# Keys turned by VectorE in 32x32 blocks, scores added from four shares, in a decode attention kernel

## The chip, the cores and the metric

The kernel runs on one core of one Trainium2 chip. The metric is the device time of one execution in microseconds (us), as the median of several runs. A profiled execution has a time of its own and a span, which goes from its first to its last instruction. The engines are TensorE (PE in the profile, its weight loads PEld), VectorE (DVE), ScalarE (ACT), GpSimd (POOL) and SyncE (SP), which here issues the large loads.

## What is computed

One decode step for two sequences: attention over a window of 4096 cached positions, with 32 query heads on 8 key/value heads of 128 elements, and a gate from a small gated MLP. All numbers are float32.

```python
W = min(4096, max(256, Sk // 4))                      # 4096
q = (x @ wq).reshape(B, Sq, Hq, Dh)                   # B = 2, Sq = 1, Hq = 32, Dh = 128
k = repeat(k_cache[:, :, Sk - W:, :], 4 heads each)
v = repeat(v_cache[:, :, Sk - W:, :], 4 heads each)
p = softmax((q . k) * Dh ** -0.5)
s = (p . v) @ wo
g = silu(gated_mlp(xn))
return x + s * g                                      # xn = layernorm(x) feeds both branches
```

## The kernel before

The loads are 89 MB: `w_in`, `w_out`, `wq`, sixteen key/value windows of 2 + 2 MB, and `wo`. They go through a ring of four slots (`slot`), all issued by SyncE in program order. A slot takes a new load when the work that read its old contents is done. The sixteen combinations of sequence and key/value head are called pairs, numbered n = 0 to 15; `load_kv(n)` puts a pair's keys and values into one slot, with position 32p + j in partition p, row j, so that each partition reads one contiguous piece. After the last pair, the ring takes `wo` in six loads.

Every engine runs its instructions in the order in which the program issues them (the class `InOrder` keeps it), so the order of the calls in the loop over `pairs` is the order on each engine. In the iteration of pair `cur`, with `prev` the pair before it and `old` the one before that, the kernel does this:

- `bias(prev)` (VectorE) and `probs(prev)` (ScalarE): the row maximum becomes the bias of the exponential, which also adds up its row (`l`).
- `transposes(cur, c)`, c = 0 to 7: TensorE transposes four 128x128 blocks of keys into a PSUM bank, and VectorE or ScalarE (`ON_ACT`) copies the bank to `kts`, one tile for each half r of the pair.
- `probs_t(prev, r)`: VectorE turns the probabilities in 32x32 blocks. `share_sum` and `weights` make the factors 1/sum.
- `scores(cur, r)`: four products, one for each quarter of the positions, each with a 32-column block of the queries `qT` as weights. The four write different quarters of the partitions of `s`, and run beside each other in the array.
- `collect(old)`: the outputs of `old` are added into `col`. When a set of heads is complete (SETS: heads 0 to 3, 4 and 5, 6 and 7 of each sequence) VectorE reduces `col` into `o1`.
- `pv(prev, r)`: probabilities times values, into `acc`; `row_max(cur)` (VectorE) and `share_max(cur)` (TensorE, into `mo`) stand around it, and `evacuate(prev)` (ScalarE) scales `acc` into `o`.

So row maximum and its shares come at the end of a pair's own iteration, and the exponential at the start of the next one. The tiles `s`, `mo` and `acc` exist once, `kts`, `o`, `p` and `pT` twice, the PSUM banks of `bank` three times.

After the loop come the bias, exponential and values of the last pair, `spread(i)`, which brings the outputs of a set into the layout for `wo`, and the product with `wo`: the first 24 rows by `wo_early` in 512-wide products into `part`, then `parts`, its copy in SBUF, is added up by products with `rowm` into `so`, where the last eight rows of `wo` go directly. `res` multiplies by the gate and adds x.

Ahead of the loop, the queries are projected (`queries(k)`, k = 0 to 3, into `pq`), copied by VectorE into `qs`, transposed by TensorE and copied into `qT`.

Of the kernel before, what the change touches and what calls it, by code (L numbers as in the profile page):

```python
# [9 lines left out]
F32 = mybir.dt.float32  # L10
# [6 lines left out]
G = 4  # L17
# [24 lines left out]
def kernel(  # L42
# [82 lines left out]
    qT = cst.tile([P, B * HKV, 32], F32, tag="qT", name="qT")  # L125
    nc.gpsimd.memset(qT, 0.0)
# [32 lines left out]
    dve.tensor_copy(same, free_ap(rowm, 0, [[0, G], [1, 32]]))  # L159
    heads = cst.tile([P, 32, REP], F32, tag="heads", name="heads")  # L160
# [101 lines left out]
    qs = sb.tile([P, NR, REP, DH], F32, tag="kts", name="qs")  # L262
    for r in range(NR):
        dve.tensor_copy(qs[:, r], pq[:, r, :].rearrange("p (i d) -> p i d", i=REP))
    for r in range(NR):
        pt = bank(f"qT_ps{r}", REP, G, 32)
        for i in range(REP):
            pe.transpose(pt[:, i].rearrange("p g c -> p (g c)"), qs[:, r, i, :], ident)
        for b in range(B):
            dve.tensor_copy(  # L270
                qT[:, b * HKV + r * G : b * HKV + r * G + G, ::8], pt[:, :, :, b].rearrange("p i g -> p g i")
            )
# [5 lines left out]
    NP = B * HKV  # L278
# [14 lines left out]
    ON_ACT = {2, 4, 5, 7}  # L293

# [3 lines left out]
    def transposes(p, c):  # L298
        r, q = divmod(c, 4)
        if q == 0:  # L300
            p.kt[r] = sb.tile([P, JH, P], F32, tag="kts", name=f"kts{p.n}_{r}")
        pk = bank(f"kt{p.n}_{c}", 4, P)
        for jj in range(4):
            pe.transpose(pk[:, jj, :], p.k[:, 4 * c + jj, :], ident)
        dst = p.kt[r][:, 4 * q : 4 * q + 4, :]
        if c in ON_ACT:
            act.activation(dst, pk, AF.Copy)
        else:
            dve.tensor_copy(dst, pk)

    def scores(p, r):
        if r == 0:
            p.s = ps.tile([P, NR, 512], F32, tag="s", name=f"s{p.n}")
        for g in range(G):
            pe.matmul(
                p.s[32 * g : 32 * g + 32, r, :], qT[:, p.n, :], p.kt[r][:, :, 32 * g : 32 * g + 32],
                start=True, stop=True,
            )
# [84 lines left out]
    for n in range(NP):  # L403
        p = Pair()
        p.n, p.kt = n, {}
        pairs.append(p)
    old = prev = None
    for cur in pairs:
        cur.k, cur.v = load_kv(cur.n)
        do(bias, prev)  # L410
        do(probs, prev)
        for c in range(4):
            do(transposes, cur, c)
        do(probs_t, prev, 0)
        do(transposes, cur, 4)
        do(transposes, cur, 5)
        do(probs_t, prev, 1)
        do(transposes, cur, 6)
# [104 lines left out]
```

## Time and profile before

| | |
|---|---|
| median of 3 runs (lowest, highest) | 219.39 us (219.15, 219.85) |
| the profiled execution: its time, its span | 219.26 us, 217.4 us |
| mean granted TensorE clock | 0.953 |
| busy: TensorE, its weight loads | 174.4 us, 105.9 us |
| busy: VectorE, ScalarE | 109.4 us, 80.5 us |
| share of the 16 DMA engines taken by SyncE's loads | 96.5% |
| read from HBM | 89.40 MB, 411 GB/s over the span |
| VectorE copies of keys out of PSUM | 64 of 680 ns, 42.2 us |
| ScalarE copies of keys out of PSUM | 64 of 597 ns, 36.8 us |
| score products | 256 records of 598 ns, 30.8 us |

The profile of one execution gives for each engine its busy time, the groups of instructions that cost most, with the mean duration of one, and what ended the idle time before them. All engine work is issued through one helper, so every group has the same line, L36, and is told apart by the tiles that it writes and reads (`kt<-ident,kv` writes `kt` and reads `ident` and `kv`). A float32 product makes two matmul records in the trace, a transpose one. Records of products that use different quarters of the array overlap, so their busy time is less than their number times their duration. In a table by windows, each row gives the start and end of a stretch, its length, busy time and instructions of the engines (PE, PEld, DVE, ACT, POOL), then the granted TensorE clock, the busy share of the DMA engines and GB/s. The chain of waits follows the execution back from its last instruction, at each step to what released it; its rows give start, length and what.

### The profile page before, as it was taken

What the parts mean: (1) busy time and instruction counts of PE and PEld (TensorE: products, weight loads), DVE (VectorE), ACT (ScalarE), POOL (GpSimd) and SP (SyncE); (2) the same over time, 40 slices, a digit from 0 to 9 for tenths busy, and PEclk for the clock granted to TensorE, in tenths of its full rate; (3) what the DMA queues carried; (4) which work ended last, traced back from release to release, by engine and by line L of the source; (5) the groups of instructions that cost most, each with busy time, mean ns of one, the idle gap of its engine ahead of it and who ended that gap; (6) DMA issues with size and microseconds to landing.
All of it is one profiled execution on the core that took longest, in us unless ns stands there. A gap on an engine that the chain in (4) does not pass through costs nothing.

```text
span 217.4 us, 3786 instructions
## 1 busy us (share of the span) xinstructions
PE 174.4 (80%) x1554; PEld 105.9 (49%) x1554; DVE 109.4 (50%) x259; ACT 80.5 (37%) x173; POOL 3.6 (2%) x17
## 2 busy tenths in 40 slices
PE   0179793977998979797977979797987899599973
PEld 0128520563663736455462736455472846384333
DVE  2411212284785737575665737575664557374201
ACT  5011203012563644435363544536363336444210
POOL 6000000000000000000000000000000000000000
PEclk9998579799999999999999999999999699969999
DMA  7999999999999999999999999999999999999980
GB/s 254 428 435 470 398 467 389 428 428 427 434 434 425 434 427 425 431 428 431 425 431 428 434 434 428 431 427 431 428 431 428 431 430 428 440 467 395 410 329 13
DMA packets 6096, 89.64 MB, mean 412 GB/s; under 512 B 686, under 2 KB 702, under 8 KB 1088
## 3 DMA queue, kind: packets, MB, share of 16 engines
q1 hardware_dynamic: 6060, 89.40, 96.5%
q8 instruction: 12, 0.20, 0.3%
q14 instruction: 4, 0.03, 0.0%
q10 hardware_dynamic: 20, 0.01, 0.0%
HBM read 89.40 MB, written 0.00 MB: 411 GB/s over the span
## 4 chain that ended last, share of the span: by engine, by line
DMA 68%; PE 27%; DVE 2%; ACT 1%; issue 1%; SPq 1%; ACTq 0%
DMA kv<-in_A_k_cache_dram 52%; DMA wq<-in_A_wq_dram 16%; PE kt L36 10%; PE s L36 4%; PE acc L36 4%; PE part L36 3%; PE q_ps L36 2%; PE y L36 1%; PE so L36 1%; PE col L36 1%; SPq L36 1%; ACT o L36 1%; DVE m L36 1%; ACT p L36 1%; PE oT_ps L36 0%
## 5 line engine op out<-in xcount | busy, mean ns | idle before, releaser
L36 PE MATMUL kt<-ident,kv 128*128 128x128 f32 x512 | 68.7, 287 | 17.5 <-DMA kv<-in_A_k_cache_dram 17.3
L36 PEld LDWEIGHTS kt<-ident,kv 128*128 128x128 f32 x512 | 58.2, 146 | 25.7 <-issue 18.0
L36 DVE COPY kts<-kt 128x512 f32<-128x512 f32 x64 | 42.2, 680 | 27.2 <-PE kt L36 18.1
L36 ACT ACTIVATE kts<-kt 128x512 f32<-128x512 f32 x64 | 36.8, 597 | 34.1 <-PE kt L36 34.1
L36 ACT ACTIVATE o<-acc,wd 128x128 f32<-128x128 f32 x64 | 18.3, 368 | 52.7 <-PE acc L36 36.0
L36 PE MATMUL s<-kts,qT 128*32 128x512 f32 x256 | 30.8, 598 | 0.0
L36 PE MATMUL acc<-kv,pT 128*16 128x512 f32 x256 | 30.4, 592 | 0.4 <-DVE pT L36 0.4
L36 DVE TENSOR_REDUCE m<-s 128x1 f32<-128x1024 f32 x16 | 19.5, 1221 | 13.5 <-PE s L36 13.5
L36 DVE STREAM_TRANSPOSE pT<-p 128x512 f32<-128x512 f32 x32 | 20.7, 685 | 0.2 <-ACT p L36 0.2
L36 ACT ACTIVATE p<-s,nb 128x1024 f32<-128x1024 f32 x16 | 18.1, 1132 | 3.7 <-DVE nb L36 3.7
L36 PE MATMUL q_ps<-wq,xnT 128*32 128x512 f32 x64 | 10.5, 789 | 5.5 <-DMA wq<-in_A_wq_dram 5.5
L36 PEld LDWEIGHTS acc<-kv,pT 128*16 128x16 f32 x256 | 7.8, 108 | 10.7 <-issue 9.8
L36 PEld LDWEIGHTS mo<-mg,same 128*128 128x128 f32 x32 | 4.8, 188 | 15.9 <-DVE mg L36 15.9
L36 PEld LDWEIGHTS s<-kts,qT 128*32 128x32 f32 x256 | 6.6, 108 | 10.0 <-ACT kts L36 7.8
L36 PE MATMUL z<-win,xnT 128*32 128x448 f32 x32 | 5.5, 862 | 4.4 <-DMA win<-in_B_w_in_dram 4.4
L36 PEld LDWEIGHTS col<-o,selw 128*32 128x32 f32 x128 | 4.1, 110 | 8.9 <-issue 8.9
L36 DVE TENSOR_REDUCE o<-col 128x32 f32<-128x128 f32 x6 | 1.7, 291 | 12.5 <-PE col L36 12.5
L36 PE MATMUL mo<-mg,same 128*128 128x4 f32 x32 | 6.2, 263 | 2.1 <-DVE mg L36 1.6
L36 DVE TENSOR_REDUCE nb<-mo 128x1 f32<-128x4 f32 x16 | 2.6, 162 | 9.9 <-PE mo L36 9.9
L36 PE MATMUL zT_ps<-rowm,z 128*128 128x2 f32 x28 | 6.6, 370 | 0.0
L36 PEld LDWEIGHTS zT_ps<-rowm,z 128*128 128x128 f32 x28 | 6.5, 325 | 0.0
L36 PE MATMUL col<-o,selw 128*32 128x128 f32 x128 | 6.5, 273 | 0.0
(98 smaller groups left out, 83.3 us busy)
## 6 DMA issues: line engine op xcount, KB each, us to landing
kv<-in_A_k_cache_dram SPq DMA_DIRECT2D x16, 2048.0 KB
kv<-in_A_v_cache_dram SPq DMA_DIRECT2D x16, 2048.0 KB, 25.4
wq<-in_A_wq_dram SPq DMA_DIRECT2D x2, 4096.0 KB, 34.1
wo<-in_A_wo_dram SPq DMA_DIRECT2D x1, 4096.0 KB
win<-in_B_w_in_dram SPq DMA_DIRECT2D x1, 3584.0 KB, 11.1
wo<-in_A_wo_dram SPq DMA_DIRECT2D x1, 2048.0 KB, 21.7
wout<-in_B_w_out_dram SPq DMA_DIRECT2D x1, 1792.0 KB, 15.0
wo<-in_A_wo_dram SPq DMA_DIRECT2D x1, 1024.0 KB
```

The costliest lines, as they stand in the source:

```text
L36: return self.tc.keep_in_program_order(call(*args, **kwargs))
```

## The change

Keys are no longer transposed by TensorE. `turn(p, q)` lets VectorE transpose the 32x32 blocks of eight rows of keys (128x1024) at once, from SBUF to SBUF, into the same `kts` tiles. What stands in partition 32g + d of a turned block is then element d of a quarter c of the head, for the positions of partition group g, so a product over all 128 partitions with the right weights mixes nothing only if the weights are zero outside one group: `qb` holds the queries spread in this way, with one 32-column block for each quarter c. `shares(p, r)` makes four products, one for each quarter of the head, into four quarters of the partitions of one bank `sh`; `keep` copies it to `ss` in SBUF (ScalarE); `scores(p, r)` is now a single product of `ss` with the 0/1 matrix `sums`, which adds the four quarters and puts the result where it was before. The queries go through ScalarE copies, VectorE transposes, a masked product (`qa`) and masked copies into `qb`, in place of TensorE transposes.

The order in the loop is new: `row_max` and `share_max` of `prev` and `collect(old)` come after the first turn of `cur`, and `bias` and `probs` of `prev` after the second. After the loop, `collect(old)` comes before the two `spread`s, `wo_early` takes a range of rows, so that four rows come ahead of the last `collect`, eight ahead of `spread(2)` and the others behind it, and the products with `parts` come after the first of the direct blocks.

```diff
--- before.py
+++ after.py
@@ -122,8 +122,10 @@
     nc.gpsimd.memset(ones, 1.0)
     hT = cst.tile([P, FT, 32], F32, tag="hT", name="hT")
     nc.gpsimd.memset(hT, 0.0)
-    qT = cst.tile([P, B * HKV, 32], F32, tag="qT", name="qT")
-    nc.gpsimd.memset(qT, 0.0)
+    qb = cst.tile([P, B * HKV, G, 32], F32, tag="qb", name="qb")
+    nc.gpsimd.memset(qb, 0.0)
+    sums = cst.tile([P, G, 4, 8], F32, tag="sums", name="sums")
+    nc.gpsimd.memset(sums, 0.0)
 
     rowm = cst.tile([P, 32], F32, tag="rowm", name="rowm")
     dve.tensor_reduce(rowm, ident.rearrange("p (g c) -> p c g", g=G), axis=AX.X, op=ALU.add)
@@ -157,6 +159,7 @@
 
     same = cst.tile([P, G, 32], F32, tag="same", name="same")
     dve.tensor_copy(same, free_ap(rowm, 0, [[0, G], [1, 32]]))
+    dve.tensor_copy(sums[:, :, :, 0], rowm[:, : G * REP].rearrange("p (g i) -> p g i", g=G))
     heads = cst.tile([P, 32, REP], F32, tag="heads", name="heads")
     dve.tensor_copy(heads, free_ap(rowm, 0, [[0, 32], [8, REP]]))
     diag = cst.tile([P, 4], F32, tag="diag", name="diag")
@@ -259,23 +262,38 @@
     dve.tensor_mul(gate, gate, y)
 
     queries(3)
-    qs = sb.tile([P, NR, REP, DH], F32, tag="kts", name="qs")
+
+
+    NP = B * HKV
+    HC = REP * G
+    qs = sb.tile([P, NR, 512], F32, tag="kts", name="qs")
+    qx = sb.tile([P, NR, HC, 32], F32, tag="kts", name="qx")
     for r in range(NR):
-        dve.tensor_copy(qs[:, r], pq[:, r, :].rearrange("p (i d) -> p i d", i=REP))
-    for r in range(NR):
-        pt = bank(f"qT_ps{r}", REP, G, 32)
-        for i in range(REP):
-            pe.transpose(pt[:, i].rearrange("p g c -> p (g c)"), qs[:, r, i, :], ident)
-        for b in range(B):
-            dve.tensor_copy(
-                qT[:, b * HKV + r * G : b * HKV + r * G + G, ::8], pt[:, :, :, b].rearrange("p i g -> p g i")
-            )
-
-
-
-
-
-    NP = B * HKV
+        act.activation(qs[:, r], pq[:, r], AF.Copy)
+        dve.transpose(qx[:, r].rearrange("p a b -> p (a b)"), qs[:, r])
+    xm = cst.tile([P, B, NR, G, HC], F32, tag="xm", name="xm")
+    for b in range(B):
+        dve.tensor_tensor(
+            xm[:, b], free_ap(qx, b, [[32 * HC, NR], [0, G], [32, HC]]), free_ap(grpm, 0, [[0, NR], [1, G], [0, HC]]),
+            op=ALU.mult,
+        )
+    qa = bank("qa", NP, REP, G)
+    pe.matmul(
+        qa.rearrange("p n i c -> p (n i c)"), same.rearrange("p g c -> p (g c)"), xm.rearrange("p b r g a -> p (b r g a)"),
+        start=True, stop=True,
+    )
+    for g in range(G):
+        dst = free_ap(qb, REP * g, [[G * 32, NP], [1, REP], [32, G]])
+        if g % 2:
+            act.activation(dst, qa, AF.Copy, scale=grpm[:, g : g + 1])
+        else:
+            dve.tensor_scalar_mul(dst, qa, grpm[:, g : g + 1])
+
+
+
+
+
+
     JH = NT // NR
     acc = ps.tile([P, 4, DH], F32, tag="acc", name="acc")
     dve.memset(acc, 0.0)
@@ -290,32 +308,35 @@
             sets[kv + a] = (a, n, o1)
         sets[f"oT{i}"] = (o1, oT, nj)
 
-    ON_ACT = {2, 4, 5, 7}
-
     class Pair:
         pass
 
-    def transposes(p, c):
-        r, q = divmod(c, 4)
-        if q == 0:
+    def turn(p, q):
+        r, a = divmod(q, 2)
+        if a == 0:
             p.kt[r] = sb.tile([P, JH, P], F32, tag="kts", name=f"kts{p.n}_{r}")
-        pk = bank(f"kt{p.n}_{c}", 4, P)
-        for jj in range(4):
-            pe.transpose(pk[:, jj, :], p.k[:, 4 * c + jj, :], ident)
-        dst = p.kt[r][:, 4 * q : 4 * q + 4, :]
-        if c in ON_ACT:
-            act.activation(dst, pk, AF.Copy)
-        else:
-            dve.tensor_copy(dst, pk)
+        n = JH // 2
+        dve.transpose(
+            p.kt[r][:, n * a : n * a + n].rearrange("p j d -> p (j d)"),
+            p.k[:, n * q : n * q + n].rearrange("p j d -> p (j d)"),
+        )
+
+    def shares(p, r):
+        p.sh[r] = bank(f"sh{p.n}_{r}", 512)
+        for c in range(G):
+            pe.matmul(
+                p.sh[r][32 * c : 32 * c + 32, :], qb[:, p.n, c, :], p.kt[r][:, :, 32 * c : 32 * c + 32],
+                start=True, stop=True,
+            )
+
+    def keep(p, r):
+        p.ss[r] = sb.tile([P, 512], F32, tag="ss", name=f"ss{p.n}_{r}")
+        act.activation(p.ss[r], p.sh[r], AF.Copy)
 
     def scores(p, r):
         if r == 0:
             p.s = ps.tile([P, NR, 512], F32, tag="s", name=f"s{p.n}")
-        for g in range(G):
-            pe.matmul(
-                p.s[32 * g : 32 * g + 32, r, :], qT[:, p.n, :], p.kt[r][:, :, 32 * g : 32 * g + 32],
-                start=True, stop=True,
-            )
+        pe.matmul(p.s[:, r, :], sums.rearrange("p g i x -> p (g i x)"), p.ss[r], start=True, stop=True)
 
     def row_max(p):
         p.m = sb.tile([P, 1], F32, tag="m", name=f"m{p.n}")
@@ -402,30 +423,32 @@
     pairs = []
     for n in range(NP):
         p = Pair()
-        p.n, p.kt = n, {}
+        p.n, p.kt, p.sh, p.ss = n, {}, {}, {}
         pairs.append(p)
     old = prev = None
     for cur in pairs:
         cur.k, cur.v = load_kv(cur.n)
+        do(turn, cur, 0)
+        do(row_max, prev)
+        do(share_max, prev)
+        do(collect, old)
+        do(turn, cur, 1)
         do(bias, prev)
         do(probs, prev)
-        for c in range(4):
-            do(transposes, cur, c)
+        do(shares, cur, 0)
+        do(keep, cur, 0)
+        do(turn, cur, 2)
+        do(turn, cur, 3)
+        do(share_sum, prev)
+        do(scores, cur, 0)
+        do(shares, cur, 1)
+        do(keep, cur, 1)
         do(probs_t, prev, 0)
-        do(transposes, cur, 4)
-        do(transposes, cur, 5)
         do(probs_t, prev, 1)
-        do(transposes, cur, 6)
-        do(transposes, cur, 7)
-        do(share_sum, prev)
         do(weights, prev)
-        do(scores, cur, 0)
         do(scores, cur, 1)
-        do(collect, old)
         do(pv, prev, 0)
-        do(row_max, cur)
         do(pv, prev, 1)
-        do(share_max, cur)
         do(evacuate, prev)
         old, prev = prev, cur
 
@@ -447,10 +470,10 @@
     EARLY = 24
     done = 0
 
-    def wo_early(n):
+    def wo_early(n, a0, a1):
         nonlocal done
         t, oT, j = blocks[n]
-        for a in range(t.shape[1]):
+        for a in range(a0, a1):
             g = done % G
             pe.matmul(
                 part[32 * g : 32 * g + 32, :], oT[:, j + a, :], t[:, a, :], start=(done < G), stop=(done >= EARLY - G)
@@ -458,35 +481,42 @@
             done += 1
 
     last = pairs[-1]
+    row_max(last)
+    share_max(last)
+    collect(old)
     bias(last)
     probs(last)
     spread(0)
     spread(1)
     probs_t(last, 0)
     probs_t(last, 1)
-    collect(old)
     share_sum(last)
     weights(last)
     part = ps.tile([P, NR, 512], F32, tag="s", name="part")[:, 0, :]
     pv(last, 0)
     pv(last, 1)
     evacuate(last)
-    wo_early(0)
+    wo_early(0, 0, 4)
     collect(last)
+    wo_early(0, 4, 12)
     spread(2)
-    wo_early(1)
+    wo_early(0, 12, 16)
+    wo_early(1, 0, 8)
     parts = sb.tile([P, D], F32, tag="o", name="parts")
     act.activation(parts, part, AF.Copy)
     so = bank("so", DC)
-    for g in range(G):
-        pe.matmul(so[32 * g : 32 * g + 32, :], rowm, parts[:, g * DC : (g + 1) * DC], start=True, stop=False)
     for n in range(2, len(blocks)):
         t, oT, j = blocks[n]
         for a in range(t.shape[1]):
             for g in range(G):
                 pe.matmul(
                     so[32 * g : 32 * g + 32, :], oT[:, j + a, :], t[:, a, g * DC : (g + 1) * DC],
-                    start=False, stop=(j + a == oT.shape[1] - 1),
+                    start=(j + a == 0), stop=(j + a == oT.shape[1] - 1),
+                )
+        if n == 2:
+            for g in range(G):
+                pe.matmul(
+                    so[32 * g : 32 * g + 32, :], rowm, parts[:, g * DC : (g + 1) * DC], start=False, stop=False
                 )
     res = cst.tile([P, DC], F32, tag="res", name="res")
     dve.tensor_mul(res, so, gate)
```

## The prediction

> **What bounds the kernel now.** I read the page first, then the chain of waits, the time line of the last 30 us, and the busy time by windows.
>
> ```profile
> DMA  7999999999999999999999999999999999999980
> GB/s 254 428 435 470 398 467 389 428 428 427 434 434 425 434 427 425 431 428 431 425 431 428 434 434 428 431 427 431 428 431 428 431 430 428 440 467 395 410 329 13
> L36 PE MATMUL kt<-ident,kv 128*128 128x128 f32 x512 | 68.7, 287 | 17.5 <-DMA kv<-in_A_k_cache_dram 17.3
> L36 DVE STREAM_TRANSPOSE pT<-p 128x512 f32<-128x512 f32 x32 | 20.7, 685 | 0.2 <-ACT p L36 0.2
> ```
>
> The DMA rows are full from the first slice to the 38th: the kernel is paced by its 89 MB of loads. Once it is running, TensorE begins each pair by waiting for that pair's keys (the kt row: 17.3 us in all, about 1.3 us per pair). In the time line the pairs start at 71.13, 80.80, ..., 148.86, 158.58, so keys arrive every 9.72 us; the last three start at 169.15, 178.83 and 189.38. Before the loads run dry, less compute buys nothing. Only what comes after the last keys (landed at 189.25 by the chain) counts:
>
> ```profile
> 166.68 22.57 DMA kv<-in_A_k_cache_dram
> 189.25 0.14 issue
> 189.38 5.48 PE kt L36 x32
> 194.86 0.12 PE mo L36 x2
> 194.98 1.85 PE s L36 x16
> ...
> 197.41 1.14 DVE m L36
> ...
> 199.98 1.10 ACT p L36 x2
> ...
> 201.87 1.92 PE acc L36 x16
> ...
> 207.53 0.25 PE col L36 x8
> ...
> 214.09 0.30 DVE res L36
> ```
>
> From landing to the last VectorE instruction (ending 214.71) is 25.5 us. The loads themselves run until about 213 (55 GB/s in 212 to 213, 4 in the next), so the end could move forward by some 0.8 us at most: 213.0, then the last output row's products (0.2) and `res` (0.65). Backward it can move freely.
>
> **The clock.** The granted clock changes on a fixed grid of 3.413 us (changes at 37.16, 40.57, 170.28, 173.69, 190.76, 194.17):
>
> ```profile
> 33.74:37.16 3.42, 0.80 (x8) 0.29 (x12) 1.30 (x7) 0.78 (x2) 0.00 (x0) 1.00 0.86 369
> 37.16:40.57 3.41, 3.41 (x44) 1.97 (x40) 0.00 (x0) 0.00 (x0) 0.00 (x0) 0.50 1.00 428
> 50.81:54.22 3.41, 1.80 (x17) 0.95 (x10) 1.77 (x4) 0.08 (x1) 0.00 (x0) 1.00 0.99 420
> 54.22:57.64 3.42, 3.42 (x30) 2.91 (x28) 3.23 (x6) 2.70 (x5) 0.00 (x0) 1.00 1.00 426
> 166.86:170.28 3.42, 1.20 (x12) 1.16 (x12) 0.71 (x3) 2.07 (x6) 0.00 (x0) 1.00 1.01 431
> 170.28:173.69 3.41, 3.41 (x19) 3.27 (x18) 2.80 (x5) 1.39 (x3) 0.00 (x0) 0.50 1.01 432
> 187.35:190.76 3.41, 1.38 (x12) 1.29 (x12) 0.83 (x4) 1.83 (x5) 0.00 (x0) 1.00 1.10 471
> 190.76:194.17 3.41, 3.41 (x18) 3.31 (x17) 2.55 (x5) 1.64 (x3) 0.00 (x0) 0.50 1.04 447
> ```
>
> After a window with TensorE busy for 0.80, 1.20 or 1.38 us (23, 35, 40%) the next window runs at half clock; after 1.80 (53%) it does not. The cut lies between. Pair 15's transposes fell in such a window: 5.48 us instead of the usual 4.14.
>
> **The change part by part.** Gone for each pair: 32 transposes (4.14 us of TensorE), four VectorE copies of 0.68 and four ScalarE copies of 0.60.
>
> *Turns.* Four VectorE transposes of 128x1024. The trace has 128x512 only: 685 ns, two in 1.29. Bounds: 0.61 (size costs nothing) to 1.37 (all of it proportional). VectorE's reductions grow by (1221-174)/1008 = 1.04 ns per element (1024 and 16 elements), so I take 0.685 + 0.533 = 1.22, a little less back to back.
>
> *Shares* are the same eight records as today's scores (16 records in 1.92): 0.86 us of TensorE, 1.03 to the end. *Keep*: ScalarE, 0.60 (row of 597 ns). *Sums*, 128 columns wide, 512 long, isn't in the trace. A record of 128 elements takes 273 ns, one of 512 takes 592, so 0.43 us of streaming for each of two records: 0.86 and 1.03 again. Bounds 0.43 (one record) and 1.56 (two of 592 and two weight loads of 188, nothing overlapped).
>
> *Start.* The query chain (two ScalarE copies, two VectorE transposes, two products, `qa`, four writes of `qb`) delays the first keys' work from 45.5 to about 47.3; copies instead of transposes save nothing. It is hidden: pair 3 waits for its keys at 71. Without that cover it costs 1.8.
>
> *The loads' queue.* A slot is freed by `pv`, which now ends some 11 us after the next pair's keys land, instead of 8.2. Everything behind it on SyncE (later keys, then `wo`) is issued 3 us later. The last keys are issued 22.6 us ahead of landing and need 4.9 for their own transfer, so 17.7 us of lateness is covered: nothing. Beyond that it would cost one for one.
>
> *Row maximum moved.* Until now a pair's `row_max`, `share_max`, `bias` and `probs` ran while TensorE waited for the next keys. Now `row_max(prev)` stands on VectorE behind `turn(cur,0)`, which waits for those keys, and the other turns stand behind it. So the loop is row_max 1.22, mg 0.26, turn 1.2, bias 0.34, two turns 2.4, shares 1.1, keep 0.65, sums 1.1, then the next row_max: about 8.7 us with its waits, against 9.72.
>
> *Collect moved.* In five pairs (5, 7, 9, 13, 15: behind the ones that end a set) VectorE also meets the reduction of `col` ahead of the second turn. It waits for `collect`, hence for `evacuate` of the pair before: 0.8 us of standing and 0.3 of work, and the late evacuate makes it about 10.9.
>
> *After the last keys*, at full clock: turn to 190.6, row_max(14) and mg to 192.1, share_max and collect to 192.8, the reduction to 193.1, turn to 194.3, bias 194.65, two turns to 197.05. Shares(15,1) follow sums(15,0) on TensorE: 197.5 to 198.55; keep 199.2; sums 200.3; row_max(15) and mg 201.8; share_max behind pv(14) and bias to 202.65. ScalarE is then at evacuate(14) until 203.2, so probs(15) ends at 204.45 (today 201.1). `probs_t` also stands behind the copies of `spread(0)` and `spread(1)`, now issued after collect(14): it starts at 205.4 instead of 201.1, 4.3 later. pv(15) to 208.0, evacuate to 209.2. Here the new split helps: four rows of `wo` instead of sixteen (0.91 instead of 3.64) precede collect(15), so that starts at 209.25 (today 207.3, 1.9 later), 8 rows 211.1, spread(2) 212.25, 12 rows 214.9. Block 2 covers the `parts` copy, saving the 0.7 us gap seen at 211.2, and products end at 217.2 instead of 214.07. Sum at full clock: **+3.2 us**.
>
> *The gate.* Between pv(13), ending near 190.3, and sums(15,0) at 196.6 TensorE has only share_max 0.4, collect 0.4, four shares 1.0 and share_sum 0.3: 2.1 of 6.3 us. A window wholly inside (2.9 of 3.41 positions) is 20 to 40% busy, and the next one runs at half clock: up to 1.7 us lost in sums, shares, sums. The same stretch recurs in all five set-ending pairs: 10.9 + 1.7 = 12.6. Against 9.72, pairs 5, 7 and 9 run up 3 x 2.9 - 2 x 1.0 = 6.7; pairs 10 to 12 give back 3.1; pair 13 adds 2.0 (its keys come 10.57 after the last), pair 14 gives back 1.0: 4.6. At full clock row_max(14) has 2.0 to spare, so 2.6 reaches pair 15, which adds 1.7: **+4.3 us**. Bounds: 0 and about 7.
>
> The Trainium skill, page "TensorE: Matmul & The Clock Gate", Part 1, has the same free-running window of about 3.4 us, but asks for an idle window before the clock falls. By that rule none of these windows would fall, since each holds some products, and the sum would be +3.2 alone; here 23 to 40% busy was enough, and I go by the rows.
>
> Sum: 3.2 + 4.3 = +7.5 on the profiled execution's 219.26 (span 217.4, 1.9 around it; 0.1 under the median of 219.39): **226.8 us**.
>
> **Rivals.**
> 1. *The clock stays full.* The busy share of windows that I work out is a hand schedule, and where a window starts differs between executions. Against: the three windows shown. 219.3 + 3.2 = 222.5.
> 2. *The loop becomes the bound.* In the other pairs the thin stretch is about 5.2 us, so a window fits in about half. Eight such pairs at 8.7 + 1.7 = 10.4, half of them, add some 6 us of arrears that nothing gives back: 232.8 (230 to 238; a sums product of 1.2 us does the same). For: a spare 1.0 us per pair is little. Against: sums and shares fill those pairs better.
> 3. *Not slower: cheap turns.* Four turns lie between the last keys and the last shares. For: one size alone is in the trace, so their growth is an inference. At 0.55 us each (4 x 0.67 = 2.7 saved, full clock) the time would be within 0.3% (0.66 us, about what a measurement here can tell) of today's; below 0.4 it is faster, down to the loads' floor at 218.6. Against: every VectorE row grows with its elements.
>
> That the transposes don't vanish is no rival: the built program has none left.
>
> **How the numbers follow.** Forecast 0.47 (its own range 224 to 229.5), full clock 0.24, loop 0.19, cheap turns 0.10. The range 220.5 to 233 leaves out most of the last and half of the loop's. Faster 0.06 and same 0.05 come from the cheap turns and the edge of the full clock; slower 0.89.
>
> **What would show it.** Turns near 1.2 us; sums records near 592 ns, two per product; the gap from the last keys' landing to `probs_t` of pair 15 at 16 us or more (today 11.85); the `col` reduction idle on TensorE ahead of turn 1; half-clock windows in pairs 5, 7, 9, 13, 15. The DMA row still full until `wo` has landed. Wrong if turns take 0.6 us, if the clock never falls after a thin window (then 222.5), or if DMA idles before slice 38 (then the loop is the bound).

## The result and the profile after

The changed kernel takes 251.23 us (median of 4 runs, 250.22 to 254.31) against 219.35 us for the kernel before on the same chip: 1.1434 times as long, 95% interval 1.1393 to 1.1475. Here and below, where the runs of one kernel scatter, a ratio is made from the undisturbed ones among them, so it can differ from that of the medians. The profiled execution took 251.11 us with a span of 248.4 us, 31.0 us more than the span before. The forecast was 226.8 us with a range of 220.5 to 233: the direction was right, the size was not, and the time lies outside the range.

From the page of the changed kernel, in the order of its parts: the rows by slices, the shares of the chain of waits, and three of the costliest groups.

```profile
PEclk9996597857559999959995798597999979955999
DMA  7999999999986999999999499969999998996000
...
PE 58%; ACT 16%; DMA 14%; DVE 7%; issue 2%; SPq 1%; ACTq 0%; DVEq 0%
...
L36 DVE STREAM_TRANSPOSE kts<-kv 128x1024 f32<-128x1024 f32 x64 | 77.0, 1226 | 0.0
L36 PE MATMUL s<-ss,sums 128*128 128x512 f32 x64 | 46.3, 812 | 18.7 <-ACT ss L36 18.6
...
L36 PE MATMUL col<-o,selw 128*32 128x128 f32 x128 | 6.8, 285 | 14.7 <-ACT o L36 14.7
```

The clock row and the shares of the chain of the kernel before:

```profile
PEclk9998579799999999999999999999999699969999
...
DMA 68%; PE 27%; DVE 2%; ACT 1%; issue 1%; SPq 1%; ACTq 0%
```

The DMA row has holes (4 and 6 in the middle), where before it was full to slice 38. The turns stand idle before them for 0.0 us: no turn ever waits for keys, they have always landed by then. The chain of waits is now TensorE and ScalarE; DMA fell from 68% of it to 14%. The loop bounds the kernel, not the loads. And the clock row dips again and again.

The starts of `evacuate`, one per iteration, divide the loss. The first stands at 75.81 us (before 61.42), the fifteenth at 229.85 (198.84), and from there to the last `res` it is 15.85 us (15.87). So 14.4 us are lost ahead of the loop's second pair, 16.6 in the loop, none behind it.

**The loop at full clock.** From the chain of waits of the changed kernel, one pair without a completed set (start, length, what):

```profile
141.04 1.15 ACT o L36 x4
...
142.23 0.43 PE col L36 x8
142.66 0.90 PE sh L36 x8
...
143.65 0.61 ACT ss L36
...
144.29 1.12 PE s L36 x2
145.42 1.04 PE sh L36 x8
...
146.54 0.61 ACT ss L36
...
147.19 1.13 PE s L36 x2
148.32 1.90 PE acc L36 x16
...
150.24 0.88 ACT o L36 x3
```

From `evacuate` to `evacuate` it is 9.20 us: evacuate, collect, shares, keep, sums, shares, keep, sums, values. `collect(old)` is ahead of the first `shares` on TensorE and waits for `evacuate`, so the shares of the next pair wait for it too, although they need nothing from it. In the time line TensorE is idle by 0.95 us before every `collect` (14.7 us in the group above).

**The clock.** Five pairs are longer. From the busy time by windows of the changed kernel, through one of them (126.04 to 141.04, 15.0 us); columns as in the table of the prediction:

```profile
122.88:126.29 3.41, 3.30 (x20) 1.01 (x20) 1.45 (x2) 0.31 (x2) 0.00 (x0) 1.00 1.00 423
126.29:129.70 3.41, 0.90 (x15) 0.32 (x16) 1.94 (x5) 1.15 (x5) 0.00 (x0) 1.00 0.99 413
129.70:133.11 3.41, 3.19 (x12) 1.00 (x4) 3.38 (x7) 1.54 (x3) 0.00 (x0) 0.50 1.03 442
133.11:136.53 3.42, 2.65 (x10) 0.51 (x10) 1.22 (x2) 0.60 (x1) 0.00 (x0) 0.50 1.00 426
136.53:139.94 3.41, 3.41 (x14) 0.54 (x17) 1.57 (x3) 0.00 (x0) 0.00 (x0) 0.50 0.53 226
139.94:143.35 3.41, 2.46 (x30) 0.77 (x22) 3.03 (x5) 2.24 (x6) 0.00 (x0) 1.00 0.44 101
```

The window with the stop is 26% busy; then three windows run at half clock, not one. The first of them is 93% busy and the second 78%, and full clock comes back only behind the third. What stops TensorE is seen in VectorE's time line of the same pair:

```profile
125.42 0.23 DVE L36 TENSOR_SCALAR mg<-grpm,m 128x4 f32<-128x4 f32 x1
127.73 0.29 DVE L36 TENSOR_REDUCE o<-col 128x32 f32<-128x128 f32 x1 [2.08 <-PE col L36]
127.94 1.23 DVE L36 STREAM_TRANSPOSE kts<-kv 128x1024 f32<-128x1024 f32 x1
```

VectorE stands 2.08 us for `collect`, and the second turn, which the first shares need, starts behind the reduction. The pairs like this are 13.4, 15.0, 13.5, 12.6 and 15.0 us long, and they are 5, 7, 9, 13 and 15; the others take 9.20, but for pair 10 with 10.84. Fourteen pairs at 9.20 would have taken 128.8 us, 8.6 less than this stretch of the loop before (137.4). The five long ones cost 23.6 us more than that and pair 10 another 1.6, which together makes the 16.6 lost in the loop.

**The start.** Windows of the changed kernel around the first pair:

```profile
44.37:47.78 3.41, 0.67 (x2) 0.30 (x2) 2.52 (x5) 0.42 (x1) 0.00 (x0) 1.00 1.00 428
47.78:51.19 3.41, 0.00 (x0) 0.00 (x0) 2.48 (x5) 1.38 (x2) 0.00 (x0) 0.50 1.02 437
51.19:54.60 3.41, 1.94 (x8) 0.23 (x8) 3.41 (x4) 0.35 (x1) 0.00 (x0) 0.50 1.00 428
...
68.25:71.67 3.42, 2.64 (x10) 0.50 (x2) 0.00 (x0) 0.60 (x1) 0.00 (x0) 0.50 1.00 426
71.67:75.08 3.41, 3.41 (x14) 0.49 (x16) 2.31 (x3) 0.00 (x0) 0.00 (x0) 0.50 0.61 259
```

While the queries are spread into `qb` (to 50.0) and pair 0 is turned (first shares at 52.26), TensorE has nothing to do. The first pairs then run at half clock (47.78 to 58.02 and 61.43 to 75.08), so the slots come free late: in the last window shown the DMA engines are down to 259 GB/s.

### The profile page after: what moved, and what is told of

Same layout as the page of the kernel before. It is cut to its first block, busy times and chain, and to the rows that moved or that the text cites. A ratio compares the mean times of both kernels' runs of the same rounds, so it can differ in the third digit from the quotient of the medians.

```text
span 248.4 us, 2838 instructions
## 1 busy us (share of the span) xinstructions
PE 175.2 (71%) x1100; PEld 57.8 (23%) x1100; DVE 141.0 (57%) x260; ACT 66.0 (27%) x145; POOL 5.0 (2%) x18
## 4 chain that ended last, share of the span: by engine, by line
PE 58%; ACT 16%; DMA 14%; DVE 7%; issue 2%; SPq 1%; ACTq 0%; DVEq 0%
PE s L36 19%; PE sh L36 17%; DMA wq<-in_A_wq_dram 14%; PE acc L36 13%; ACT ss L36 8%; ACT o L36 7%; DVE kts L36 4%; PE col L36 3%; PE q_ps L36 2%; PE part L36 2%; PE oT_ps L36 1%; PE y L36 1%; PE so L36 1%; DVE o L36 1%; DVE qx L36 1%
## 5 line engine op out<-in xcount | busy, mean ns | idle before, releaser
L36 DVE STREAM_TRANSPOSE kts<-kv 128x1024 f32<-128x1024 f32 x64 | 77.0, 1226 | 0.0
L36 PE MATMUL s<-ss,sums 128*128 128x512 f32 x64 | 46.3, 812 | 18.7 <-ACT ss L36 18.6
L36 PE MATMUL sh<-kts,qb 128*32 128x512 f32 x256 | 44.3, 772 | 13.6 <-DVE nb L36 8.5
L36 ACT ACTIVATE ss<-sh 128x512 f32<-128x512 f32 x32 | 19.1, 597 | 60.2 <-PE sh L36 60.2
L36 PE MATMUL acc<-kv,pT 128*16 128x512 f32 x256 | 33.6, 645 | 0.7 <-DVE pT L36 0.7
L36 PEld LDWEIGHTS s<-ss,sums 128*128 128x128 f32 x64 | 11.6, 227 | 41.9 <-ACT ss L36 39.4
L36 PE MATMUL col<-o,selw 128*32 128x128 f32 x128 | 6.8, 285 | 14.7 <-ACT o L36 14.7
L36 PE MATMUL q_ps<-wq,xnT 128*32 128x512 f32 x64 | 10.6, 790 | 5.5 <-DMA wq<-in_A_wq_dram 5.5
L36 PEld LDWEIGHTS sh<-kts,qb 128*32 128x32 f32 x256 | 6.3, 120 | 33.5 <-DVE wd L36 10.5
L36 PEld LDWEIGHTS acc<-kv,pT 128*16 128x16 f32 x256 | 6.8, 114 | 26.3 <-issue 25.0
L36 PEld LDWEIGHTS mo<-l,heads 128*128 128x128 f32 x32 | 5.8, 227 | 16.5 <-ACT p L36 16.5
L36 PE MATMUL mo<-l,heads 128*128 128x1 f32 x32 | 7.1, 292 | 0.4 <-ACT p L36 0.4
## 6 DMA issues: line engine op xcount, KB each, us to landing
kv<-in_A_v_cache_dram SPq DMA_DIRECT2D x16, 2048.0 KB, 14.1
```

Of the source, the lines that this page charges most:

```text
L36: return self.tc.keep_in_program_order(call(*args, **kwargs))
```

## The experiments

The theory after the result was: the loop is now the bound, and most of the loss is half clock behind thin windows; the rivals were the new order as such, the place of `collect`, the start, and the tail. "Filler" below is a product of 128x384 that is written to PSUM and read by nobody; it only keeps TensorE busy.

**Fillers in the thin stretches.** `fill(t, k)` issues k products; eight stand ahead of pair 0, and in the loop:

```diff
         do(share_max, prev)
+        if prev is not None:
+            fill(prev.mo, 1)
         do(collect, old)
+        if old is not None and old.n % HKV in (3, 5, 7):
+            fill(prev.mo, 2)
...
         do(weights, prev)
+        if prev is not None:
+            fill(prev.mo, 1)
         do(scores, cur, 1)
```

> The changed kernel with filler products on TensorE, whose results nobody reads: eight ahead of the first pair, one behind each share_max, one ahead of the second sums product, two more behind collect in the pairs after a set is complete. Clock theory (the loop is slow because thin windows halve the clock, and a half clock then lasts two or three windows): the windows stay above 60% busy, the clock stays full after the first pair, plain pairs take 9.2 to 9.7 us, pairs behind a set's end about 11 instead of 12.6 to 15.0, and the time falls from 251 to 222-228 us. Order theory (the loop through pv, evacuate, collect, shares is too long at any clock, the clock only follows the idle time): the fillers add work to a loop that is already the bound, and the time stays above 240 us.

Measured: 233.6 us (230.89 to 234.82), ratio 1.0569 (1.0526 to 1.0613). The time lies between the two readings, some 6 us above the first. The pairs behind a completed set took 11.2 us instead of 12.6 to 15.0, as the clock theory had it, the others 9.20 as before. The first `evacuate` still came at 74.55.

With more fillers behind pair 0's products as well:

```diff
-            fill(prev.mo, 1)
+            fill(prev.mo, 2 if prev.n == 0 else 1)
...
         do(scores, cur, 1)
+        if prev is None:
+            fill(f0, 4)
```

> As e1_warm, with the start kept busy too: four more fillers behind pair 0's second sums product, two instead of one behind its share_max. In e1_warm the windows from 61.4 to 71.6 us still ran at half clock and the first evacuate came at 74.6 us. Clock theory: no half clock from 51 us on, the first evacuate at 66-68 us, then 9.2 us per plain pair and 11.2 behind a set's end as in e1_warm, so the loads set the pace again: 221-226 us. If the cold start is hidden by the loads' queue anyway, it stays at e1_warm's 231-233 us.

Measured: 233.09 us (232.12 to 233.72), ratio 1.0614 (1.0562 to 1.0666). The 221 to 226 us were missed, and the run before is not told from this one by its interval. The only half clock left behind the start is 214.88 to 218.29. So without the gate about 18 of the 31.9 us go, although added work stands in the loop. The other 13.8 are at the start (first `evacuate` 72.23 us, 10.8 late), in the loop (1.5) and behind it (1.4): the loop at 9.20 and 11.2 us per pair gives nothing back.

With fillers behind completed sets only:

```diff
         do(collect, old)
+        if old is not None and old.n % HKV in (3, 5, 7):
+            fill(prev.mo, 3)
```

> The changed kernel with three fillers behind collect in the pairs behind a set's end (5, 7, 9, 13, 15) and nowhere else. In the changed kernel these five pairs took 13.4, 15.0, 13.5, 12.6 and 15.0 us, the others 9.2 (pair 10: 10.8). If the thin window there is what drops the clock, they come to about 11.2 each, 13 us less in all, and the time falls to 236-241 us, with the cold start left. If other stretches drop the clock as well, half-clock windows move to other pairs and the time stays above 246 us.

Measured: 241.82 us (240.68 to 242.64), ratio 1.1013 (1.0965 to 1.106). The five pairs took 11.8 to 11.9 us, the others 9.2; half clock was left only at the start and at 222.6 to 226.05. The time is just above the 236 to 241 us that were expected: the fillers write to `mo`, which `bias` reads, and 2.15 us of them stand on the chain of waits ahead of it, so these pairs are longer than the 11.2 of the run with fewer fillers there. So the thin windows of these five pairs alone are worth 9.4 us net of the fillers.

**The old order with the turns.** `row_max` and `share_max` back at the end of the iteration, `bias` and `probs` at its start, `collect` ahead of the values:

```diff
+        do(bias, prev)
+        do(probs, prev)
         do(turn, cur, 0)
-        do(row_max, prev)
-        do(share_max, prev)
-        do(collect, old)
         do(turn, cur, 1)
-        do(bias, prev)
-        do(probs, prev)
...
         do(scores, cur, 1)
+        do(collect, old)
         do(pv, prev, 0)
+        do(row_max, cur)
         do(pv, prev, 1)
+        do(share_max, cur)
```

> The changed kernel with the old order of the loop: row_max and share_max of a pair at the end of its own iteration, bias and probs at the start of the next, collect between the second sums product and pv. Turns, shares, keep and sums stay. Order theory: no evacuate or collect stands ahead of shares any more, every pair has time to wait for its keys, the loads stay full, and what is left is the tail: four turns 4.8, shares 1.04, keep 0.65, sums 1.12 from the last keys to the row maximum, some 7.9 us against 7.6 before; 217 to 224 us. Clock theory alone: TensorE is idle for longer in front of each pair's first shares than in the changed kernel, so half-clock windows come in more pairs, not fewer, and the time stays above 235 us.

Measured: 290.62 us (288.54 to 291.62), ratio 1.3224. The theory of the order fell: the new order is much the better one for these turns. Windows of this run, one pair:

```profile
119.41:122.83 3.42, 1.04 (x10) 0.30 (x2) 2.49 (x5) 2.24 (x6) 0.00 (x0) 1.00 0.49 110
122.83:126.24 3.41, 2.80 (x11) 1.06 (x12) 3.41 (x5) 0.60 (x1) 0.00 (x0) 0.50 0.99 423
126.24:129.65 3.41, 3.41 (x10) 0.35 (x9) 0.60 (x3) 0.00 (x0) 0.00 (x0) 0.50 1.04 447
129.65:133.07 3.42, 2.63 (x26) 0.93 (x26) 0.93 (x2) 0.60 (x1) 0.00 (x0) 1.00 0.58 249
```

Every pair takes 13.65 us, which is four windows of 3.413: one thin (30%), two at half clock, one at full clock, and again. The loop is locked to the clock's grid. The same with fillers behind `bias` and ahead of the second sums, and eight ahead of pair 0:

```diff
         do(bias, prev)
         do(probs, prev)
         do(turn, cur, 0)
         do(turn, cur, 1)
+        if prev is not None:
+            fill(prev.mo, 4)
         do(shares, cur, 0)
...
         do(weights, prev)
+        if prev is not None:
+            fill(prev.mo, 1)
         do(scores, cur, 1)
```

> e2_order_back with fillers: eight ahead of pair 0, four between each pair's bias and its first shares, one ahead of the second sums product. e2_order_back took 13.65 us in every pair, which is four windows of the clock, with two of four at half clock. Clock theory: with the gap filled the clock stays full, a pair takes 9.5 to 10.2 us (row maximum and bias 2.1, four turns 4.6, shares, keep and sums 2.9), and the time falls from 290 to 222-232 us. If the old order itself costs 13.65 us, nothing changes: above 280 us.

Measured: 253.82 us (253.6 to 254.22), ratio 1.1565, 11.3 us per pair without half clock. This is more than the 222 to 232 us of the clock theory, and far below the 280 of the other reading. The four fillers stand on the chain of waits (2.85 us), but the two turns beside them take 2.4, so they add about 0.5 us at most. So the old order costs some 11 us per pair at full clock: between the values of one pair and the shares of the next stand `share_max`, `bias` and two turns in a row.

**Only the place of collect.** First between the second sums and the values:

```diff
         do(share_max, prev)
-        do(collect, old)
...
         do(scores, cur, 1)
+        do(collect, old)
         do(pv, prev, 0)
```

> The changed kernel with one call moved: collect(old) back between the second sums product and pv, where it was before. Row maximum stays behind the first turn. If the loop through evacuate and collect is what binds, plain pairs fall from 9.2 to about 8.3 us at full clock, the extra stop in the pairs behind a set's end goes, and the time falls to 224-234 us. If thin windows bind by themselves, share_max to shares is still thin (0.4 us busy in about 3), the half clock still comes, and the time stays within 245-255 us.

Measured: 244.87 us (244.36 to 245.24), ratio 1.1164. The loop is shorter at full clock, 8.94 us (8.3 was expected), but thin windows stayed. Now the reduction meets the pair one later: pairs 8, 10 and 14 took 14.3 to 14.6 us, and pairs 2, 3 and 6 took 10.4 to 10.6. With fillers added to this version:

```diff
         do(share_max, prev)
+        if prev is not None:
+            fill(prev.mo, 3 if prev.n == 0 else 1)
...
         do(weights, prev)
+        if prev is not None:
+            fill(prev.mo, 1)
         do(scores, cur, 1)
+        if prev is None:
+            fill(f0, 4)
         do(collect, old)
         do(pv, prev, 0)
         do(pv, prev, 1)
+        if prev is not None:
+            fill(prev.mo, 1)
```

> The changed kernel with collect moved back as in e3_collect_late and TensorE kept busy: fillers ahead of pair 0 and behind its scores, one behind each pv, one behind each share_max (three in pair 1), one ahead of the second sums product. At full clock e3_collect_late took 8.94 us per pair, below the 9.72 us between keys. If clock and loop are both understood, all pairs keep pace with the keys, the loads are full to their end, and only the tail behind the last keys is longer than before by 0 to 3 us: 218.5-223 us. If something else binds (VectorE's own work, a buffer), pairs stay above 9.72 us and the time above 226 us.

Measured: 239.07 us (238.5 to 241.24), ratio 1.0913, without half clock in the loop, but 10.3 us per pair: a miss of the experiment. The fillers write to `mo`, and `bias`, which reads it, waited for them (1.47 us before it in VectorE's time line), so this run says nothing of the loop.

Then behind the fourth turn, so that TensorE meets `collect` when `evacuate` is long done, and the reduction stands behind all turns:

```diff
         do(share_max, prev)
-        do(collect, old)
         do(turn, cur, 1)
...
         do(turn, cur, 3)
+        do(collect, old)
         do(share_sum, prev)
```

> The changed kernel with collect(old) moved from ahead of the first shares to behind the fourth turn, so that TensorE no longer waits for evacuate ahead of the first shares and the reduction of col stands behind all turns. If the loop at full clock runs through evacuate, collect and shares, a plain pair takes 8.9 us and not 9.2 (8.94 where collect stood between the second sums and the values), and the set-ending pairs no longer stand out by the 2.0 us of the reduction. If the clock gate then still takes its windows (it falls below some 60% busy in a window of 3.41 us and comes back only after a nearly full one), two to four half-clock stretches stay, at other places than the five set-ending pairs: 228 to 240 us. If the set-ending stop was the only cause of the thin windows in the loop, none stays behind pair 4: 222 to 228 us. The first evacuate stays at about 75 us in both.

Measured: 226.19 us (223.24 to 228.03), ratio 1.0199 (1.0179 to 1.0219). One call moved takes 25.0 of the 31.9 us away, by the medians. The profiled execution took 226.80 us. From the page of this run, and from TensorE's time line in the pair from 109.35 to 118.1:

```profile
PEclk9996587965557999999999999999999659998598
DMA  7999999999999699999999999999999999999900
```

```profile
110.19 1.07 PE L36 MATMUL sh<-kts,qb 128*32 128x512 f32 x8 [0.56 <-DVE nb L36]
111.07 0.40 PE L36 MATMUL col<-o,selw 128*32 128x128 f32 x8
```

`collect` no longer waits, and the pairs take 8.73 us, those behind a completed set too. The chain of waits of this pair runs through ScalarE's `evacuate`, `probs` and `keep`, and then sums, shares, keep, sums and values. Between 70 and 176 us the clock is full without any filler, and the DMA row is full again but for one slice. The loop gives time back until pairs wait for their keys (9.8 and 9.7 us, then one with half clock of 14.1): 13.1 us late at the first `evacuate`, 5.5 at the fifteenth, 7.6 at the end, where pair 15's values ran at half clock (3.62 us in place of 1.92).

**The start moved as well.** On top of that, the turns of pair 0 ahead of the product `y`, the gate's arithmetic behind the queries' chain, and six fillers around pair 0's shares and sums:

```diff
+    pairs[0].k, pairs[0].v = load_kv(0)
+    for q in range(4):
+        turn(pairs[0], q)
     y = bank("y", DC)
...
     dve.memset(acc, 0.0)
+    gate = cst.tile([P, DC], F32, tag="gate", name="gate")
...
+    f0 = ps.tile([P, 512], F32, tag="mo", name="fill")
+    fill(f0, 4)
     old = prev = None
     for cur in pairs:
...
         do(scores, cur, 1)
+        if prev is None:
+            fill(f0, 2)
```

> As the run before it, and pair 0's four turns stand ahead of the MLP's last product, the gate's VectorE and ScalarE work behind the queries' chain, with four filler products ahead of pair 0's shares and two behind its second sums (written to mo, read by nothing). If the start's loss is the chain queries, spreading, four turns, shares of pair 0 plus the half clock that the gap brings, the first evacuate comes at 64 to 69 us in place of 75 (61.4 in the kernel before), the fourth slot's reload comes by as much earlier, and the time is 6 to 10 us under the run before it: 219 to 230 us. If the start does not matter because the loop catches up, the two runs agree within 2 us.

Measured: 221.24 us in the profiled execution, 226.23 to 226.92 in three others; so by the median (226.29) nothing was gained on the run before it, where 6 to 10 us were expected; only its shortest time is 2.0 us below the shortest of that run (223.24). What follows is of the shortest execution, the only one profiled. Its first `evacuate` came at 69.89 us, a little later than expected, and the DMA engines never ran dry: they move 409 to 459 GB/s in every slice from the second to the 38th. One half-clock stretch was left in the loop (134.47 to 144.71), behind a window that was 56% busy. From VectorE's time line of this execution:

```profile
187.71 1.25 DVE L36 STREAM_TRANSPOSE kts<-kv 128x1024 f32<-128x1024 f32 x1 [1.94 <-DMA kv<-in_A_k_cache_dram]
...
202.70 1.29 DVE L36 STREAM_TRANSPOSE pT<-p 128x512 f32<-128x512 f32 x2
...
216.32 0.29 DVE L36 TENSOR_TENSOR res<-res,x 128x128 f32<-128x128 f32 x1
```

Here the last keys set the end again. From their landing to the end it is 28.9 us, against 25.5 in the kernel before.

Then fillers into banks of their own, one behind each `share_max` and three ahead of the values behind a completed set; in the second run of this pair only the three:

```diff
         do(share_max, prev)
+        if prev:
+            fill(bank(f"fa{cur.n}", 512), 1)
...
         do(scores, cur, 1)
+        if old and sets[old.n % HKV][0] == sets[old.n % HKV][1] - 1:
+            fill(bank(f"fb{cur.n}", 512), 3)
         do(pv, prev, 0)
```

> As the run with the early start, with one filler product of 128x384 behind each share_max and three more ahead of the values where a set of heads has just been completed, into banks of their own that nobody reads. In the run with the early start the loop turned at 8.75 us per pair, under the 9.72 of the loads, but one half-clock stretch of 10 us (134 to 145) stood behind a window that was 56% busy, and its four times lay from 221.2 to 226.9. If that half clock is all that still separates it from the kernel before, no half clock is left between 60 and 200 us, the four or more times lie within 1 us of each other, and the time is 218.5 to 220.5 us: no different from the kernel before, since the loads set the end. If the fillers lie on the loop's own chain (8.75 + 0.65 to 9.4 us per pair) it is 219 to 222 us. Something else in the loop would give 222 to 228 us.

> As the run before it, with the three fillers behind a completed set only. If the thin windows of the early-start kernel stand at the completed sets alone, it equals the run before it within 0.5 us; if they come also where a pair waits for its keys (TensorE idle by 1 us of 9.7), half-clock stretches stay and it is 1 to 7 us above it, with times apart by several us.

Measured: 223.3 us (223.1 to 223.46), ratio 1.017 (1.0151 to 1.0189), and 224.16 us (223.48 to 225.06), ratio 1.0215 (1.0179 to 1.025). The clock is full from 53.3 to 206.9 us in the first, and the four times lie within 0.4 us: the scatter of the two kernels before it is gone, together with the half clock in their loops. But the three fillers lie on the loop's own chain, as its row shows:

```profile
198.25 1.94 PE fb L36 x6
200.18 1.90 PE acc L36 x16
```

The five pairs take 10.7 us, the others 8.7, and no wait for keys is left in the loop's part of the chain. From 8.9 us late at the first `evacuate` (70.3) the kernel is still 3.3 late at the fifteenth (202.1) and 4.3 at the end. It missed the 218.5 to 220.5 of the first reading, came out 1.3 us above the second, and lies in the range that was left for something else in the loop; what the rows show there is the longer five pairs (10.7 where 8.75 to 9.4 were reckoned). The other run has a half-clock window at 63.6 to 67.0; it is 0.9 us longer, between its two readings, and the intervals of the two touch.

**The changed tail alone, on the kernel before.** `wo_early` in ranges and the products with `parts` behind the first direct block:

```diff
-    wo_early(0)
+    wo_early(0, 0, 4)
     collect(last)
+    wo_early(0, 4, 12)
     spread(2)
-    wo_early(1)
+    wo_early(0, 12, 16)
+    wo_early(1, 0, 8)
```

> The kernel before with the changed tail alone: four rows of wo ahead of the last collect, eight ahead of spread(2), the parts products behind the first direct block. The prediction put the saving at some 2.6 us less TensorE work ahead of the last collect and 0.7 us of gap at parts, but the last loads land near 213 us: if they are the floor, the gain is 0.4 to 0.9 us; if the products with wo alone fill the tail, none, because the same rows come later.

Measured: 219.18 us (218.73 to 219.4), ratio 0.9991 (0.9982 to 1.0). The end of its chain of waits:

```profile
189.29 23.98 DMA wo<-in_A_wo_dram
...
213.32 0.47 PE so L36 x8
```

The last load of `wo` lands at 213.28 and sets the end, whatever the tail does: the new split is worth 0.2 us there by the medians, which the interval does not tell from nothing; the 0.4 to 0.9 us of the one reading did not come. No version tried is faster than the kernel before by more than can be measured.

## Why the prediction was wrong, point by point

- *Turns, shares, keep*: right. The turn was put at 1.22 us and took 1226 ns; keep at 0.60 and took 597 ns; shares at 1.03 us to the end and took 1.04 at full clock.
- *Sums*: put at 0.86 of TensorE and 1.03 to the end; measured 1.12 to the end, and the next product starts 1.06 behind it (144.29 to 145.35). Mis-sized, twice per pair.
- *Row maximum moved, "about 8.7 us with its waits"*: this step failed. The working went around through `row_max` and the turns, and counted `collect` only in the five pairs where VectorE meets its reduction. But `collect(old)` stands ahead of the first shares on TensorE in every pair and waits for ScalarE's `evacuate`, so the loop went through evacuate, collect and shares: 9.20 us. Where only this call was moved, the pair took 8.73. That this is so near the 8.7 of the working is luck: its chain goes through `evacuate`, `probs` and `keep` on ScalarE and touches neither `row_max` nor the turns. Against the loads' 9.72 the loop gave back 0.5 us per pair instead of 1.0, and together with the five long pairs less than nothing.
- *Collect moved*: the five pairs were the right ones, and 10.9 us for them at full clock was near: 11.2 with fillers. But VectorE stood 2.08 us where 0.8 was reckoned, in a loop that was longer for another reason.
- *The gate*: the thin windows came in these five pairs (and one in pair 10), but "up to 1.7 us lost" in one window each was the term that was mis-sized. The rows before showed one half-clock window at a time, because there TensorE had 32 transposes waiting and filled it. The changed loop has waits between shares, keep and sums, so a half-clock window is often only 57 to 93% busy, and the clock stays down for two or three windows: 13.4, 15.0, 13.5, 12.6 and 15.0 us, 69.6 in all and 6.6 above five times 12.6. At the 11.2 us of the run with fillers the five would take 56.1, so 13.5 us of them are half clock, where five times 1.7 were reckoned.
- *Start, "1.8 us, hidden"*: failed twice. The chain through `qb` and four turns leaves TensorE without work for more than one window, which brings half clock to the first pairs; that was not looked at. And the cover, pair 3 waiting for its keys, exists only while the loop is faster than the loads. It was not, and the prediction's own terms leave little room: pairs 2 to 4 can make up 3 us, and over the whole loop nine pairs of 8.7 with five of 12.6 make 141.3 us, more than the 137.4 of the loop before. So all 14.4 us reached the end. With the loop at 8.73 they partly came back: 13.1 late at the start, 7.6 at the end.
- *The loads' queue, "nothing"*: failed with it. `pv` of pair 0 ended so late that the next slot was issued at 75.81 in place of 61.41, and the DMA engines ran dry. 17.7 us of cover were for a lateness of 3, not of 14 and growing.
- *After the last keys, +3.2*: not seen in the changed kernel, where the loads no longer set the end. Where they did again (the early start), landing to end was 28.9 in place of 25.5 us: +3.4, of which 1.4 is pair 15's values at half clock (3.28 against 1.92), so about +2.0 without it. From landing to `probs_t` it was 15.0 us, where 16 or more were to show the prediction right.
- The rival of the loop as the bound (232.8, 230 to 238) was the right kind of outcome at a fifth of the chance, and too small: its half clock was looked for in the plain pairs, where only one fell (pair 10), and it had neither the start nor the second and third half-clock window. The prediction's own test, DMA idle ahead of slice 38, told it apart at once.

The Trainium skill, page "TensorE: Matmul & The Clock Gate", Part 1, lets the clock fall after an idle window and rise after a busy window of about 3.4 us. The grid of 3.413 us agrees. The fall does not: windows of 0.90 and 1.04 us of products (26 and 30%) were enough here. On the return the rows ask for more than that one sentence: a window of 3.19 us busy (93%) did not bring it back at 133.11.

What stays open is why just the move behind the fourth turn, and not the one between sums and values, keeps nearly all windows above the cut; only the result of both is shown. And whether a filler small enough to leave the loop's slack would bring the early start down to the time before was not tried.

## What to carry to other kernels

An instruction put early for one engine's sake holds up all that is behind it on every engine it uses: write down, for each engine, what the moved call waits for and what stands behind it, in every iteration and not only in those where it does most. Cover by waiting for loads is one sum for the whole kernel; before a delay is called hidden, check that the changed loop is still faster than the loads, with its long iterations averaged in. When work that kept TensorE dense goes to another engine, reckon the clock with windows of the new loop, and by the columns that its products stream: half clock here lasted until a window streamed for some three quarters of its length, and the loop's own waits can keep it from ever doing so.

## What the runs showed of the hardware

- Half clock is easily entered and hard to leave. Over the profiles of all these kernels the clock came back 85 times, 77 of these behind a window at least 90% busy; but 26 windows of 90% or more at half clock were followed by another one at half. In the loop of the changed kernel it fell behind windows 26 to 59% busy and not behind those from 60% up. Over all kernels, windows between 53 and 92% busy are found on both sides, and near 20 us each kernel fell behind a window that was full; so the cut is no single share of busy time.
- What fits these windows far better is the number of columns that the products stream. In the kernel before, a record of 128 columns took 273 ns and one of 512 took 592: 0.83 ns for a column, and some 167 ns that do not grow with them. The estimate that follows counts of each record only its columns, twice as long at half clock, and records that run beside each other once. By it full clock was lost behind 85 windows of at most 41% and kept behind 610 of at least 35%; from half clock it came back behind 85 windows of at least 73% and did not behind 94 of at most 70%. At half clock, 73% is about as many columns as 37% at full clock. The full window of the changed kernel near 20 us counts 25%, since most of it is this group of products with two columns each, and the one of 93% at 129.70 counts 67%. No run set the number of columns on purpose.

```profile
L36 PE MATMUL zT_ps<-rowm,z 128*128 128x2 f32 x28 | 6.6, 370 | 0.0
```

- A loop can lock to the grid: 13.65 us per pair, four windows of 3.413, for thirteen pairs in a row, where the same work took 11.3 with fillers.
- More products made it faster: 18 us by products that nobody reads.
- VectorE's transpose of 128x1024 float32 takes 1226 ns where 128x512 took 670 to 685: it grows with the elements, at about 1.1 ns each.
